# Sharing the first layer's weight conversion between ScalarE and VectorE in three ways

## The chip, the cores and the metric

One core of a Trainium2 chip. The metric is the device time of one execution in microseconds (us), the lower the better. TensorE multiplies matrices, ScalarE and VectorE work elementwise, GpSimd takes some elementwise work too, and SyncE's queue issues the DMA transfers.

## The reference, cut to what matters

```
attention (8 batches, 8 heads, 576 queries, 64 wide, 32 packed queries p):
    pp  = softmax(p k^T / 8) v            # 32 rows per head
    x   = softmax(q pp^T / 8) pp          # 4608 tokens x 512
layer 1:  h = x @ w_in;  g = h - tanh(h);  x = g @ w_out      # 512 -> 2048 -> 512
layer 2:  h = x @ w_in2; g = h * cos(h);   out = g @ w_out2   # float32
```

The weights arrive as 64-bit floats. The kernel has to make 32-bit floats of them on the chip, and splits each (as it does other operands) into a high part of type fp32r, which TensorE multiplies, and a low part, the rest, of the same type.

## The kernel before, in words

**Weights of layer 1.** `w_in` and `w_out` come as 16 tiles each, 32 in all, of 128 x 512 doubles (512 KB). `ORDER` (line 33) fixes their order; `i` is a tile of `w_in`, `o` one of `w_out`. The class `Conv` (line 105) takes a tile through stages. `prefetch` issues its load into the tile `st`, through SyncE's queue. `a` does ScalarE's part on the two 32-bit words of each double: line 140 scales the high word, read as a float, into the tile `w` (exponent and upper fraction bits, three places too low); line 142 makes the three lowest bits of the result from the low word; in one of two ways line 147 makes the sign. `b_ops` returns VectorE's part as a list of functions. `c` (only for `w_out`) splits into high part (ScalarE, line 185) and low part (GpSimd, line 186).

There were two ways. If `ACT_SIGN` has a 1 for the tile, line 142 writes the low bits into the lower 16-bit half of the low word and line 147 the sign, as a 16-bit float, into its upper half; VectorE then has one operation, `join` (line 164): shift `w` left by three and OR the word to it. If it has a 0, line 142 writes the whole 32-bit word, line 147 falls away, and VectorE puts in the sign (line 159) and then joins (line 164). The first 17 tiles and every second one after are of the first kind: 24 and 8. The weights of layer 2 take the second way, all of them, and much later.

**Steps.** Layer 1 runs in steps. A step is two of 16 groups of 128 hidden columns for one block of 288 tokens: `h1` (12 matmuls, line 459), `el1` (tanh and square on ScalarE, lines 474, 475), `el2` (VectorE, lines 486 to 493, with two ScalarE passes, 481 and 484), `el3` and `el4` (high part on ScalarE, line 501, and low part on VectorE, line 506), and two steps later `ymm1` (24 matmuls, line 521). VectorE's conversion functions go between those of `el2` (`fill`, line 997). `x @ w_in` is never made as such: `gmat` (line 413) multiplies the packed attention rows of a batch with `w_in` first, which needs four converted tiles of `w_in`, and `gsplit` (lines 435, 440) splits the product. The first 16 steps need the first half of both weights, the next ones the rest. The tables `PRE_A`, `PRE_B` and `STEP_A` say how many tiles are begun at each place of the program.

**Order.** The program first works on the attention of batch 0 with conversions between (`slot`), then runs the steps with the later batches' attention between them. Up to step 15 a scheduler orders each engine's queue when the program is built: by what is ready after its own durations, and by priority (the last part of batch 0's softmax has a higher one). From step 15 on each queue has the written order (`STEP_ORDERED`, line 42). Queues are served in order: an instruction that waits holds up all behind it on its engine. Scores, transposes, `gmat` and `h1` share two PSUM buffers (`psh`), and staged weights, converted weights and `gsplit`'s output share 32 buffers of the pool `wp`.

```
way "1":  ACT 140 high -> w     ACT 142 low bits -> 16-bit half   ACT 147 sign -> other half   DVE 164 join
way "0":  ACT 140 high -> w     ACT 142 low bits -> 32-bit word   DVE 159 sign                 DVE 164 join
```

Of the kernel before, what the change touches and what calls it, by code (L numbers as in the profile page):

```python
# [15 lines left out]
U32 = mybir.dt.uint32  # L16
F16 = mybir.dt.float16
BF16 = mybir.dt.bfloat16
AF = mybir.ActivationFunctionType
ALU = mybir.AluOpType  # L20
# [13 lines left out]
    "i2 i0 i3 i1 o1 o0 i4 i5 i6 i7 o3 o4 o2 o5 o7 i8 "  # L34
    "o6 i9 i10 i11 i14 o9 i12 i13 o8 i15 o11 o13 o12 o10 o15 o14"
).split()
ACT_SIGN = "11111111111111111010101010101010"
PRE_A = (0, 1, 1, 1, 1, 0, 1, 1, 1, 0, 1, 1, 0, 0, 0)
PRE_B = (1, 0, 1, 1, 2, 0, 2, 2, 0, 1, 2, 2, 0, 3, 0)
STEP_A = (1, 2, 2, 2, 1, 2, 1, 1, 1, 1, 0, 2, 1, 1, 1, 1, 1, 1, 0, 3, 1, 1)  # L40
# [12 lines left out]
SGN = -2147483648  # L53
LOW_BIAS = -0.5 + 2.0 ** -10
# [3 lines left out]
def fused_kernel(ctx, tc, qT, kT, v, pT, w1i, w1o, w2i, w2o, ident, out):  # L58
    nc = tc.nc
    B, _, _, _, HB = qT.shape  # L60
    S = 2 * HB
# [31 lines left out]
    def f32(ap):  # L93
        return ap.bitcast(F32)
# [10 lines left out]
    class Conv:  # L105
# [19 lines left out]
        def a(self):  # L125
            self.prefetch()
            if not self.ready:
                return
            kind, f, st = self.ready.pop(0)
            by_act = kind[1] == "1" and ACT_SIGN[self.na] == "1"  # L130
            self.na += 1
            if kind == "w1i":
                if f // 2 not in w1in:
                    w1in[f // 2] = wp.tile([128, 2, 512], F32, tag="w", name="w1i")
                w = w1in[f // 2][:, f % 2, :]
            else:
                w = self.alloc_tmp()
            sv = st.rearrange("p (n two) -> p n two", two=2)
            hi, x = sv[:, :, 1], sv[:, :, 0]
            nc.scalar.activation(out=w, in_=f32(hi), func=AF.Copy, scale=2.0 ** -112)  # L140
            halves = st.bitcast(U16).rearrange("p (n four) -> p n four", four=4)
            nc.scalar.activation(  # L142
                out=halves[:, :, 0] if by_act else x, in_=x.bitcast(U32), func=AF.Identity,
                scale=2.0 ** -29 * (1 - 2.0 ** -11), bias=LOW_BIAS,
            )
            if by_act:
                nc.scalar.activation(  # L147
                    out=halves[:, :, 1].bitcast(F16), in_=f32(hi), func=AF.Copy, scale=2.0 ** -60
                )
            self.done_a.append((kind, f, hi, w, x, by_act))  # L150

        def b_ops(self):
            if not self.done_a:
                return []
            kind, f, hi, w, x, by_act = self.done_a.pop(0)
            wi = w.bitcast(I32)

            def sign():
                nc.vector.scalar_tensor_tensor(
                    out=x, in0=hi, scalar=SGN, in1=x, op0=ALU.bitwise_and, op1=ALU.bitwise_or  # L160
                )

            def join():
                nc.vector.scalar_tensor_tensor(
                    out=wi, in0=wi, scalar=3, in1=x,
                    op0=ALU.logical_shift_left, op1=ALU.bitwise_or,
                )
                if kind == "w1i":
                    self.bdone.add(f)
                else:  # L170
                    self.done_b.append((kind, f, w))
                self.prefetch()

            return [join] if by_act else [sign, join]

        def b(self):
            for fn in self.b_ops():
# [563 lines left out]
    def bprep(t, bo):  # L741
# [16 lines left out]
        def sub(o, a, b):  # L758
            return lambda: nc.vector.tensor_tensor(out=o(), in0=a(), in1=b(), op=ALU.subtract)
# [273 lines left out]
    p3c, p3 = run_pool("p3")  # L1033
    pend, hist, bo, nyt, sums = [], [], {}, [], []
    seq = [(i, t, s, a, b) for i, (t, a, b) in enumerate(PARTS) for s in range(a, b)]
    nxt = [p[0] for p in PARTS[1:]]

# [200 lines left out]
```

## Time and profile before

| | |
|---|---|
| median of 3 runs | 1560.5 us (1559.47 to 1560.88) |
| profiled execution | 1559.06 us, its span 1557.2 us |
| TensorE busy | 1485.1 us (95%) |
| VectorE busy | 1115.0 us (72%) |
| ScalarE busy | 960.8 us (62%) |
| GpSimd busy | 184.4 us (12%) |

```profile
PE   3588999999999999999989999999999999999999
DVE  4598888787888878788965655567767577747661
```

The page cuts the span into 40 slices of 39 us and gives the busy share of each in tenths. TensorE is below 90% in the first four slices only. The conversion of layer 1 lies in the first five. PE is TensorE's matrix multiplication, PEld its weight load, DVE VectorE, ACT ScalarE, POOL GpSimd; PEclk is the granted clock of TensorE as a share of 2.4 GHz. Busy time counts each moment once, while the mean of a group counts an instruction's whole duration, and neighbours overlap by some 0.1 us.

### The profile page before, as it was taken

How to read it: one execution, taken by the hardware profiler on the slowest of the kernel's cores; microseconds unless marked ns; L12 is line 12 of the kernel's file. 1: busy time of each engine (PE TensorE's matmuls, PEld its weight loads, DVE VectorE, ACT ScalarE, POOL GpSimd, SP SyncE). 2: the span in 40 equal slices, each digit the busy share in tenths (PEclk: the TensorE clock that was granted, in tenths of full speed). 3: DMA queues.
4: the chain of work that ended last, by engine and by line, in shares of the span. 5: the costliest groups of instructions: out<-in, count | busy, mean ns of one | idle time of the engine just before them, and what ended most of it. 6: DMA issues, size and time to landing. Idle time of an engine off the chain costs nothing.

```text
span 1557.2 us, 25930 instructions
## 1 busy us (share of the span) xinstructions
PE 1485.1 (95%) x10192; PEld 1294.2 (83%) x10192; DVE 1115.0 (72%) x1547; ACT 960.8 (62%) x1450; POOL 184.4 (12%) x155
## 2 busy tenths in 40 slices
PE   3588999999999999999989999999999999999999
PEld 1477888999999999999978778888888888888887
DVE  4598888787888878788965655567767577747661
ACT  7998856565666757567877755555555355535541
POOL 0231101010100101011124435300000000000000
PEclk6699999999999999999999999999999999999999
DMA  9332223111212111103546742564666475647542
GB/s 342 134 130 84 92 67 106 35 62 62 66 62 64 43 37 50 62 32 113 170 144 228 239 167 95 198 233 167 236 226 259 140 257 188 260 151 280 177 172 110
DMA packets 88506, 223.54 MB, mean 144 GB/s; under 512 B 8960, under 2 KB 36608, under 8 KB 88384
## 3 DMA queue, kind: packets, MB, share of 16 engines
q1 hardware_dynamic: 88384, 221.88, 40.9%
q8 instruction: 81, 1.33, 0.4%
q14 instruction: 41, 0.34, 0.1%
HBM read 173.34 MB, written 48.50 MB: 142 GB/s over the span
## 4 chain that ended last, share of the span: by engine, by line
PE 84%; ACT 7%; DVE 4%; issue 3%; DMA 1%; POOL 1%; SPq 0%; DVEq 0%; POOLq 0%; ACTq 0%
PE y L642 24%; PE y L521 23%; PE p L791 15%; PE h L459 11%; PE h L585 7%; PE gp L421 2%; ACT st L142 2%; ACT st L147 1%; DVE y L489 1%; ACT wt L140 1%; PE pp L328 1%; DVE y L493 1%; ACT u L475 1%; DMA st<-w1i 1%; PE s L271 1%
## 5 line engine op out<-in xcount | busy, mean ns | idle before, releaser
L521 PE MATMUL y<-gh,w1o 128*128 128x288 f32 x2048 | 311.8, 304 | 11.3 <-ACT gh L501 6.3
L521 PEld LDWEIGHTS y<-gh,w1o 128*128 128x128 f32 x2048 | 285.2, 191 | 39.7 <-ACT t L474 14.5
L459 PE MATMUL h<-a,g 128*128 128x288 f32 x1536 | 229.3, 298 | 11.7 <-DVE g L440 6.3
L791 PE MATMUL p<-b,wa 128*128 128x512 f32 x1008 | 239.8, 389 | 0.0
L459 PEld LDWEIGHTS h<-a,g 128*128 128x128 f32 x1536 | 214.4, 191 | 14.4 <-ACT a L379 10.0
L791 PEld LDWEIGHTS p<-b,wa 128*128 128x128 f32 x1008 | 189.2, 188 | 39.2
L474 ACT ACTIVATE t<-h 128x576 f32<-128x576 f32 x128 | 83.6, 653 | 201.4 <-PE h L459 201.2
L642 PE MATMUL y<-wo,gh 128*128 128x512 f32 x768 | 188.1, 389 | 0.0
L642 PEld LDWEIGHTS y<-wo,gh 128*128 128x128 f32 x768 | 144.2, 188 | 29.9
L521 PE MATMUL y<-gl,w1o 128*128 128x288 f32 x1024 | 157.6, 296 | 0.5 <-DVE gl L506 0.5
L521 PEld LDWEIGHTS y<-gl,w1o 128*128 128x128 f32 x1024 | 143.2, 189 | 0.7 <-DVE gl L506 0.7
L486 DVE TENSOR_TENSOR t<-h,t 128x576 f32<-128x576 f32 x128 | 95.4, 745 | 59.7 <-ACT u L475 59.2
L585 PE MATMUL h<-yhl,w2i 128*128 128x512 f32 x576 | 134.3, 389 | 0.0
L585 PEld LDWEIGHTS h<-yhl,w2i 128*128 128x128 f32 x576 | 108.1, 188 | 22.4
L493 DVE COPY_PREDICATED y<-k,t 128x576 f32<-128x576 int16 x128 | 109.2, 854 | 12.5 <-DVE y L489 0.5
L802 ACT ACTIVATE a<-ha 128x1024 f32<-128x1024 f32 x24 | 25.5, 1062 | 140.3 <-DVE ha L799 140.3
L506 DVE TENSOR_TENSOR gl<-y,gh 128x576 fp32r<-128x576 f32 x128 | 102.0, 797 | 8.8 <-ACT gh L501 7.9
L642 PE MATMUL y<-w2o,gh 128*128 128x512 f32 x384 | 95.7, 395 | 3.9 <-DVE o L685 2.0
L489 DVE SCALAR_TENSOR_TENSOR y<-y,d 128x576 f32<-128x576 f32 x128 | 96.9, 757 | 2.3 <-ACT y L481 2.1
L642 PE MATMUL y<-wo,gl 128*128 128x512 f32 x384 | 97.8, 389 | 0.0
L487 DVE TENSOR_TENSOR d<-u,h 128x576 f32<-128x576 f32 x128 | 95.0, 742 | 0.0
L501 ACT ACTIVATE gh<-y 128x576 fp32r<-128x576 f32 x128 | 87.8, 686 | 9.1 <-DVE y L493 8.7
(116 smaller groups left out, 2118.3 us busy)
## 6 DMA issues: line engine op xcount, KB each, us to landing
wo<-wod SPq DMA_DIRECT2D x96, 512.0 KB, 6.2
wa<-wsd SPq DMA_DIRECT2D x48, 512.0 KB, 6.3
wa<-wid SPq DMA_DIRECT2D x24, 512.0 KB, 5.7
y<-ye SPq DMA_DIRECT2D x80, 144.0 KB, 1.9
out<-o SPq DMA_DIRECT2D x36, 256.0 KB, 2.2
st<-w1i SPq DMA_DIRECT2D x16, 512.0 KB, 8.0
v<-vv SPq DMA_DIRECT2D x16, 512.0 KB, 5.1
st<-w1o SPq DMA_DIRECT2D x16, 512.0 KB, 6.6
```

Of the source, the lines that this page charges most:

```text
L459: nc.tensor.matmul(out=h[:, x, 0:HB], lhsT=gw[b, f // 4, half][:, ga, c0:c0 + 128], rhs=a2[b, half][:, aa, HB * j:HB * j + HB], start=(n = ...
L474: nc.scalar.activation(out=st["t"], in_=h, func=AF.Tanh)
L486: lambda: nc.vector.tensor_tensor(out=t, in0=hs, in1=t, op=ALU.subtract),
L487: lambda: nc.vector.tensor_tensor(out=d, in0=u, in1=hs, op=ALU.mult),
L489: lambda: nc.vector.scalar_tensor_tensor(out=y, in0=y, scalar=PC0 - PC1 * PC1 / (4 * PC2), in1=d, op0=ALU.add, op1=ALU.mult,),
L493: lambda: nc.vector.copy_predicated(out=y, mask=k.bitcast(I16), data=t),
L501: nc.scalar.activation(out=st["gh"], in_=st["g"], func=AF.Copy)
L506: nc.vector.tensor_tensor(out=st["gl"], in0=st["g"], in1=f32(st["gh"]), op=ALU.subtract)
L521: nc.tensor.matmul(out=yps[blk][d][:, 0:HB], lhsT=w1out[f][:, wh, 128 * d:128 * d + 128], rhs=st[gg][:, x, :], start=(s in first and x == ...
L585: nc.tensor.matmul(out=h[:, x, :], lhsT=w2in[f][:, wa, 128 * k:128 * k + 128], rhs=yt[k][:, ya, :], start=(n == 0), stop=(n == 11),)
L642: nc.tensor.matmul(out=yps[t, lo_s][m], lhsT=st[gg][:, x, 128 * m:128 * m + 128], rhs=w[:, wh, :], start=(s == lo_s and x == 0 and not lo ...
L791: nc.tensor.matmul(out=dst, lhsT=wa[wi][:, 128 * j:128 * j + 128], rhs=b[j][:, bi, :], start=(n == 0), stop=(n == 5),)
```

## The change

A third way is added, and a string names the way of each tile: `S` is the old way 1, `L` the old way 0, and in `D` ScalarE only makes the high word; VectorE shifts it left by three in place (`shift`), puts in the sign (`put_sign`) and joins the top three bits of the untouched low word (`join`, its other branch). Of the 32 tiles 6 are S, 20 L and 6 D.

```diff
@@ -34,7 +34,7 @@
     "i2 i0 i3 i1 o1 o0 i4 i5 i6 i7 o3 o4 o2 o5 o7 i8 "
     "o6 i9 i10 i11 i14 o9 i12 i13 o8 i15 o11 o13 o12 o10 o15 o14"
 ).split()
-ACT_SIGN = "11111111111111111010101010101010"
+SPLIT = "LLSLLLSLLLSLLLSLDLSLDLDLSLDLDLDL"
 PRE_A = (0, 1, 1, 1, 1, 0, 1, 1, 1, 0, 1, 1, 0, 0, 0)
 PRE_B = (1, 0, 1, 1, 2, 0, 2, 2, 0, 1, 2, 2, 0, 3, 0)
 STEP_A = (1, 2, 2, 2, 1, 2, 1, 1, 1, 1, 0, 2, 1, 1, 1, 1, 1, 1, 0, 3, 1, 1)
@@ -127,7 +127,7 @@
             if not self.ready:
                 return
             kind, f, st = self.ready.pop(0)
-            by_act = kind[1] == "1" and ACT_SIGN[self.na] == "1"
+            way = SPLIT[self.na] if kind[1] == "1" else "L"
             self.na += 1
             if kind == "w1i":
                 if f // 2 not in w1in:
@@ -139,20 +139,21 @@
             hi, x = sv[:, :, 1], sv[:, :, 0]
             nc.scalar.activation(out=w, in_=f32(hi), func=AF.Copy, scale=2.0 ** -112)
             halves = st.bitcast(U16).rearrange("p (n four) -> p n four", four=4)
-            nc.scalar.activation(
-                out=halves[:, :, 0] if by_act else x, in_=x.bitcast(U32), func=AF.Identity,
-                scale=2.0 ** -29 * (1 - 2.0 ** -11), bias=LOW_BIAS,
-            )
-            if by_act:
+            if way != "D":
+                nc.scalar.activation(
+                    out=halves[:, :, 0] if way == "S" else x, in_=x.bitcast(U32),
+                    func=AF.Identity, scale=2.0 ** -29 * (1 - 2.0 ** -11), bias=LOW_BIAS,
+                )
+            if way == "S":
                 nc.scalar.activation(
                     out=halves[:, :, 1].bitcast(F16), in_=f32(hi), func=AF.Copy, scale=2.0 ** -60
                 )
-            self.done_a.append((kind, f, hi, w, x, by_act))
+            self.done_a.append((kind, f, hi, w, x, way))
 
         def b_ops(self):
             if not self.done_a:
                 return []
-            kind, f, hi, w, x, by_act = self.done_a.pop(0)
+            kind, f, hi, w, x, way = self.done_a.pop(0)
             wi = w.bitcast(I32)
 
             def sign():
@@ -160,18 +161,34 @@
                     out=x, in0=hi, scalar=SGN, in1=x, op0=ALU.bitwise_and, op1=ALU.bitwise_or
                 )
 
+            def shift():
+                nc.vector.tensor_scalar(
+                    out=wi, in0=wi, scalar1=3, scalar2=None, op0=ALU.logical_shift_left
+                )
+
+            def put_sign():
+                nc.vector.scalar_tensor_tensor(
+                    out=wi, in0=hi, scalar=SGN, in1=wi, op0=ALU.bitwise_and, op1=ALU.bitwise_or
+                )
+
             def join():
-                nc.vector.scalar_tensor_tensor(
-                    out=wi, in0=wi, scalar=3, in1=x,
-                    op0=ALU.logical_shift_left, op1=ALU.bitwise_or,
-                )
+                if way == "D":
+                    nc.vector.scalar_tensor_tensor(
+                        out=wi, in0=x, scalar=29, in1=wi,
+                        op0=ALU.logical_shift_right, op1=ALU.bitwise_or,
+                    )
+                else:
+                    nc.vector.scalar_tensor_tensor(
+                        out=wi, in0=wi, scalar=3, in1=x,
+                        op0=ALU.logical_shift_left, op1=ALU.bitwise_or,
+                    )
                 if kind == "w1i":
                     self.bdone.add(f)
                 else:
                     self.done_b.append((kind, f, w))
                 self.prefetch()
 
-            return [join] if by_act else [sign, join]
+            return {"S": [join], "L": [sign, join], "D": [shift, put_sign, join]}[way]
 
         def b(self):
             for fn in self.b_ops():
```

## Rows read from the trace of the kernel before

**Rows 1.** the stretches: busy us and instructions of each engine, PEclk, DMA share, GB/s

```profile
20.00:64.00 44.00, 14.76 (x131) 8.28 (x124) 26.74 (x47) 42.56 (x56) 7.29 (x5) 0.50 0.58 215
64.00:122.00 58.00, 45.47 (x422) 40.87 (x421) 49.67 (x73) 54.21 (x83) 16.32 (x11) 0.91 0.40 133
122.00:186.00 64.00, 59.68 (x492) 54.57 (x490) 55.62 (x79) 55.86 (x100) 9.59 (x7) 0.96 0.29 98
186.00:280.00 94.00, 89.82 (x912) 81.90 (x911) 80.53 (x136) 57.36 (x102) 8.80 (x7) 1.00 0.28 84
...
100.00:120.00 20.00, 15.57 (x137) 13.80 (x138) 19.27 (x31) 19.57 (x33) 6.80 (x5) 0.92 0.39 136
```

**Rows 2.** the chain of waits, 26 to 64 us: share by line

```profile
by line: ACT st L147 29.0%; ACT st L142 28.1%; PE y L521 6.7%; ACT wt L140 6.4%; ACT g L435 5.1%; ACT w1i L140 4.9%; ACT u L362 3.3%; ACT a L379 2.8%; ACT w1o L185 2.2%; ACT e L295 2.2%; DVE wt L164 1.8%; ACT gh L501 1.5%; ACT k L484 1.5%; 
```

**Rows 3.** TensorE's instructions in order: start, us, what, idle before and its releaser

```profile
40.88 3.22 PE L459 MATMUL h<-a,g 128*128 128x288 f32 x12 [6.33 <-DVE g L440]
54.39 1.96 PE L421 MATMUL gp<-w1i,pt 64*32 64x256 f32 x32 [10.29 <-ACT e L295]
...
63.86 2.66 PE L459 MATMUL h<-a,g 128*128 128x288 f32 x12
```

**Rows 4.** ScalarE's instructions in order

```profile
39.85 1.38 ACT L147 ACTIVATE st<-st 128x512 f16<-128x512 f32 x1
40.94 1.44 ACT L142 ACTIVATE st<-st 128x512 uint16<-128x512 uint32 x1
42.09 0.71 ACT L185 ACTIVATE w1o<-wt 128x512 fp32r<-128x512 f32 x1
...
54.24 0.64 ACT L474 ACTIVATE t<-h 128x576 f32<-128x576 f32 x1
...
88.27 0.69 ACT L140 ACTIVATE w1i<-st 128x512 f32<-128x512 f32 x1
88.84 0.68 ACT L142 ACTIVATE st<-st 128x512 int32<-128x512 uint32 x1
89.40 0.67 ACT L481 ACTIVATE y<-u 128x576 f32<-128x576 f32 x1
```

**Rows 5.** groups of 0 to 330 us by form: count, busy us, mean ns, idle before

```profile
L142 ACT ACTIVATE st<-st 128x512 uint16<-128x512 uint32 x24 | 32.8, 1380 | 0.0
...
L147 ACT ACTIVATE st<-st 128x512 f16<-128x512 f32 x24 | 32.6, 1369 | 0.2
...
L164 DVE SCALAR_TENSOR_TENSOR wt<-wt,st 128x512 int32<-128x512 int32 x16 | 14.0, 879 | 6.9 <-ACT st L147 3.3 <-ACT wt L140 2.7 <-DMA st<-w1o 0.8
L164 DVE SCALAR_TENSOR_TENSOR w1i<-w1i,st 128x512 int32<-128x512 int32 x16 | 11.8, 747 | 13.4 <-ACT st L147 9.4 <-ACT w1i L140 4.0
...
L159 DVE SCALAR_TENSOR_TENSOR st<-st 128x512 int32<-128x512 int32 x8 | 8.7, 1085 | 0.9 <-ACT st L142 0.9
...
L142 ACT ACTIVATE st<-st 128x512 int32<-128x512 uint32 x8 | 5.6, 705 | 0.0
```

**Rows 6.** all engines in order, 119.3 to 120.1 us

```profile
119.37 0.68 DVE L164 SCALAR_TENSOR_TENSOR w1i<-w1i,st 128x512 int32<-128x512 int32 x1
...
119.84 1.50 POOL L380 TENSOR_TENSOR a<-ut,a 128x576 fp32r<-128x576 f32 x1 [6.00 <-ACT a L379]
119.97 1.93 DVE L159 SCALAR_TENSOR_TENSOR st<-st 128x512 int32<-128x512 int32 x1
```

**Rows 7.** VectorE's one-input operations of the whole span

```profile
L685 DVE TENSOR_SCALAR o<-y 128x512 f32<-128x512 f32 x18 | 12.3, 687 | 19.9 <-PE y L642 9.6 <-POOL w2o L186 8.3 <-DMA out<-o 2.0
...
L338 DVE TENSOR_SCALAR px<-pp,sm 128x128 f32<-128x128 f32 x16 | 5.5, 341 | 4.5 <-PE pp L328 4.5
```

**Rows 8.** the sign passes (line 147) by stretch: busy us and count

```profile
0.00:54.20 54.20, 16.06 (x12) 0.64 0.81 292
...
64.00:122.00 58.00, 10.90 (x8) 0.91 0.40 133
122.00:186.00 64.00, 4.22 (x3) 0.96 0.29 98
```

## The prediction, made before the result was known

> **What bounds the kernel now.** I read the busy time by stretch first [rows 1]. From 186 us on TensorE is busy 89.8 of 94 us; nothing in this change happens there, so what counts is how much earlier or later the steps reach that stretch. Before it, in 20 to 186 us, the fullest engine is ScalarE: 42.56 of 44 us (97%), 54.21 of 58 (93%) and 55.86 of 64 (87%). VectorE has 26.74 (61%), 49.67 (86%) and 55.62 (87%). TensorE does little up to 64 us, and at a granted clock of 0.50, its 1.2 GHz level; from 64 to 122 us it is idle for 12.5 us.
>
> Then the chain of waits of 26 to 64 us [rows 2]: lines 147 and 142, ScalarE's sign and low-bits passes of the conversion, are 57% of it. TensorE's rows show what that does [rows 3]: the first h product runs at 40.88, and then TensorE waits 10.29 us for ScalarE's exp of batch 1 (which frees a PSUM buffer); the first tanh starts only at 54.24 [rows 4], though its product is done at 44.1. The second h product starts at 63.86.
>
> **What a tile costs on each engine.** By form [rows 5] the low-bits pass takes 1380 ns into the 16-bit half and 705 ns into the 32-bit word; the sign pass, 16-bit too, 1369 ns. Neighbours overlap, so I take start to start [rows 4]: sign 40.94-39.85 = 1.09, 16-bit low bits 42.09-40.94 = 1.15, high bits 88.84-88.27 = 0.57, 32-bit low bits 89.40-88.84 = 0.56. So a tile holds ScalarE for 0.57+1.15+1.09 = 2.81 us by way S, 1.13 by L, 0.57 by D.
>
> On VectorE S has one op (join), L two, D three. The two ops that exist take 680 ns undisturbed, 0.60 start to start (119.37 to 119.97) [rows 6]. But over all 40 of them the mean is (16x879 + 16x747 + 8x1085)/40 = 867 ns [rows 5], since some are stretched; less the 0.08 of overlap, 0.79 each. The sign op at 119.97 shows the stretch: 1.93 us while GpSimd's L380 runs (119.84 for 1.50) [rows 6]. The Trainium skill, "SBUF — State Buffer", section "SBUF: two separate sides", says that a VectorE op with two SBUF inputs and a GpSimd op exclude each other for a whole instruction. Rows 6 agree, and it speaks against the change: 18 of the added ops have two SBUF inputs.
>
> The shift of way D has no row: a one-input op of 512 elements, SBUF to SBUF. The nearest row is the 512-element scalar op out of PSUM, 687 ns [rows 7]; below it lies nothing but the op's fixed part, for which the 128x128 row (341 ns) is an upper bound. I take the same 0.79 as for the others; with 0.34 six shifts would save 2.7 us of VectorE, and that end I keep for the range. The Trainium skill, "VectorE: DVE Perf Modes", section "The perf-mode tier table", gives such an fp32 op two elements a cycle; by it the sum would be about 2 us lower (an estimate), and no row here shows that.
>
> **The change, stretch by stretch.** Sign passes: 24 in all [rows 5], 8 and 3 of them in the second and third stretch [rows 8], so 13 in the first; since before every tile up to number 16 and the even ones after are S, these are tiles 0-12, 13-25 and 26-31.
> - Up to 64 us: tiles 0,1,3,4,5,7,8,9,11,12 go S to L. ScalarE 10 x 1.68 = -16.8; VectorE +10 ops = +7.9.
> - 64 to 122: tiles 13, 15 to L, 16, 20, 22 to D. ScalarE 2x1.68 + 3x2.24 = -10.1; VectorE 2+6 = 8 ops, +6.3.
> - 122 to 186: tiles 26, 28, 30 to D. ScalarE -6.7; VectorE 6 ops, +4.7.
>
> Sum: ScalarE -33.6, VectorE +18.9 us. Loads, their queue, the high/low split (lines 185, 186) and TensorE's work stay as they are.
>
> Start. Twelve sign passes lie ahead of the first tanh at 54.24 [rows 8], nine of them on tiles that become L: ScalarE would be free for it 9x1.68 = 15.1 us earlier, at 39.1. The product it reads then ends last (44.1; it waits for VectorE's g and ScalarE's a, which I put 3 us earlier, so 41). So ScalarE's side would give 13 us. VectorE's side gives less: 26.74+7.9, less some 1.6 us (signs of tiles 0 and 1, whose low bits are made before 20 us) = 33.0 us of work. Filled as ScalarE was here, 97%, that takes 34.0 instead of 44 us: **-10.0**. The smaller gain counts.
>
> After it VectorE is the fullest engine. 64 to 122: 49.67+6.3 = 56.0; filled as ScalarE now is, 93%, it takes 60.2: **+2.2**. 122 to 186: 55.62+4.7 = 60.4, at the same 93% 64.9: **+0.9**. There is a row for such filling: 19.27 of 20 us (96%) in 100 to 120. TensorE needs less than that in the second stretch (45.47 busy), and about the same in the third (59.68).
>
> Sum -6.9 on the profiled execution's 1559.06 (span 1557.2 and 1.9 around it): 1552.2. The median of the runs is 1.4 above the profiled one, so 1553.5.
>
> What hides what: the added VectorE ops cost nothing only where VectorE waits for ScalarE (17 us idle in 20 to 64). If the static order sets them ahead of batch 0's softmax or of the maximum of batch 1, that cover is gone and each costs its 0.8. From step 15 the order is the written one: a D tile puts three ops between the chain's ops of a step instead of one, so the masked copy that ends it (and with it gh, y's operand) comes up to 1.6 us later; with 93% filling that is counted.
>
> **Rivals.**
> 1. *The order closes up* (22%). The passes that go were what the start waited for, and with ScalarE 20% emptier VectorE no longer waits for it: the start gives the 13 us of ScalarE's side, and the 116.4 us of VectorE work in 64 to 186 fit at 98%, 118.8 against 122. -16: 1544.5. For it: a queue as full as ScalarE's, 93 to 97%, is what each release had to pass through. Against it: 98% stands in no row.
> 2. *VectorE too full, slower* (20%). VectorE in 64 to 186 fills only as in 186 to 280, where nothing else is full: 80.53 of 94, 86%; TensorE is 4% idle there already. And the added ops meet GpSimd as the eight old sign ops did (1085 ns, 1.0 each), for GpSimd is busy 28% of 64 to 122. Then 105.3+14.0 = 119.3 at 88% is 135.6, +13.6, while the start gives 26.74+10-2 = 34.7 at 93%, 37.3, -6.7. +7: 1567; with 90% +4, 1564. It decides from below 90% filling on. For it: both engines were nearly even here and the load only changes place.
> 3. *The start is held elsewhere* (13%). Between the first tanh and the second h product 9.6 us pass through two PSUM buffers (gp of rows 3, then a transpose and scores of batch 1); if the order puts the freed time of ScalarE to later tiles instead, the start gives the 3 us of the first product only, and VectorE takes them back: within 0.2%, 1557.4 to 1563.6, which is about what a measurement can tell from no change. DMA is no such holder: busy 0.58 of 20 to 64 [rows 1].
>
> That the passes don't get shorter is excluded: 1380 against 705 ns in one line and one kernel.
>
> **How the numbers follow.** My forecast has 45%, 1553.5, its own range 1548 to 1557 (95% and 91% filling, with the shift's two ends). The rivals have 22, 20 and 13%. Faster 67%, same 13%, slower 20%. The range goes from 1542 (rival 1 with the cheap shift) to 1565 (most of rival 2).
>
> **What would show it.** In the profile after: sign passes 24 to 6, 16-bit low bits 24 to 6, 32-bit low bits 8 to 20; ScalarE some 40 us less busy, VectorE 15 to 19 more; first tanh near 42 and second h product near 54; in 64 to 175 VectorE over 92% and ScalarE under 80%. Wrong if the second h product stays near 64 (rival 3), if VectorE stays under 90% while TensorE's idle time grows after it (rival 2), or if the second stretch shortens too (rival 1). From 186 us on (by the new clock 7 earlier) everything should be as before.

## The result, and the profile after

The median is 1543.86 us (5 runs) against 1559.97 us: ratio 0.9898, 95% interval 0.9883 to 0.9912, 16 us less. Forecast were 7 us less (1553.5); the direction and the start came as forecast, the size of what follows the start did not, and the time is that of rival 1. The profiled execution took 1545.49 us, its span is 1543.6, so the traces show 13.6 of the 16 us.

In the new listing the conversion's ScalarE passes are lines 140 (high), 143 (low bits) and 148 (sign), VectorE's operations 160 (sign), 181 (join), and 165, 170, 176 (way D); all behind stands 17 lines lower. Of the page after: part 1, and two rows of part 2 (slices of 38.6 us).

```profile
PE 1486.3 (96%) x10192; PEld 1293.5 (84%) x10192; DVE 1124.2 (73%) x1571; ACT 927.1 (60%) x1426; POOL 185.2 (12%) x155
...
PE   4889999999999999999989999999999999999999
...
DVE  5899888787878878788956655567767577747661
```

VectorE's busy time over the whole run rose by 9.2 us (1115.0 to 1124.2); forecast were 15 to 19. ScalarE's fell by 33.7, which is the sum's 33.6 and not the "some 40" of its last paragraph. In 64 to 175 us VectorE is 94% busy and ScalarE 79%, as that paragraph had it.

The stretches are best cut where the same step starts: at the second h product (steps are counted from 0, so this is step 1), at that of step 9 and that of step 17. Columns as in [rows 1]: PE, PEld, VectorE, ScalarE, GpSimd, then granted clock, DMA share, GB/s. The kernel before:

```profile
20.00:63.90 43.90, 14.66 (x131) 8.18 (x124) 26.64 (x47) 42.46 (x56) 7.29 (x5) 0.50 0.58 215
63.90:128.70 64.80, 52.27 (x461) 46.58 (x461) 55.05 (x81) 58.50 (x92) 17.61 (x12) 0.88 0.36 119
128.70:171.90 43.20, 40.10 (x349) 37.02 (x347) 37.49 (x52) 39.14 (x68) 5.70 (x4) 1.00 0.33 113
```

The changed one:

```profile
20.00:55.00 35.00, 15.46 (x124) 8.69 (x125) 31.63 (x55) 27.72 (x48) 7.15 (x5) 0.50 0.71 264
55.00:114.70 59.70, 50.81 (x458) 44.92 (x458) 55.15 (x87) 48.01 (x82) 17.22 (x12) 0.88 0.37 130
114.70:157.50 42.80, 40.02 (x350) 37.09 (x348) 40.52 (x58) 35.11 (x65) 6.49 (x5) 1.00 0.36 117
```

So the three stretches shrank by 8.9, 5.1 and 0.4 us; forecast were -10.0, +2.2 and +0.9. (The forecast cut at 122 and 186 us, not at steps 9 and 17; with the nearest marks, the last matmuls of step 8's h and step 19, the second shrank by 5.0 and the third by 0.6.) VectorE's work in them (the third busy column) is 26.64, 55.05, 37.49 before and 31.63, 55.15, 40.52 after: +5.0, +0.1, +3.0, where I had +6.3, +6.3 and +4.7. Its filling is 90, 92 and 95%, where I had 97, 93 and 93%. From step 17 on 0.8 us are lost again.

The groups of 0 to 330 us by form, against [rows 5]:

```profile
L160 DVE SCALAR_TENSOR_TENSOR st<-st 128x512 int32<-128x512 int32 x20 | 15.7, 795 | 0.2 <-ACT st L143 0.2
L143 ACT ACTIVATE st<-st 128x512 int32<-128x512 uint32 x20 | 13.7, 683 | 0.1
...
L181 DVE SCALAR_TENSOR_TENSOR w1i<-w1i,st 128x512 int32<-128x512 int32 x14 | 10.6, 771 | 3.4 <-ACT w1i L140 3.4
...
L181 DVE SCALAR_TENSOR_TENSOR wt<-wt,st 128x512 int32<-128x512 int32 x12 | 9.3, 779 | 0.0
...
L143 ACT ACTIVATE st<-st 128x512 uint16<-128x512 uint32 x6 | 8.2, 1364 | 0.0
L148 ACT ACTIVATE st<-st 128x512 f16<-128x512 f32 x6 | 8.2, 1360 | 0.1
...
L165 DVE TENSOR_SCALAR wt<-wt 128x512 int32<-128x512 int32 x4 | 2.9, 736 | 0.0
...
L170 DVE SCALAR_TENSOR_TENSOR wt<-st,wt 128x512 int32<-128x512 int32 x4 | 2.7, 678 | 0.0
L176 DVE SCALAR_TENSOR_TENSOR wt<-st,wt 128x512 int32<-128x512 int32 x4 | 2.7, 677 | 0.0
...
L170 DVE SCALAR_TENSOR_TENSOR w1i<-st,w1i 128x512 int32<-128x512 int32 x2 | 1.8, 908 | 0.0
...
L176 DVE SCALAR_TENSOR_TENSOR w1i<-st,w1i 128x512 int32<-128x512 int32 x2 | 1.4, 681 | 0.0
...
L165 DVE TENSOR_SCALAR w1i<-w1i 128x512 int32<-128x512 int32 x2 | 0.8, 410 | 0.0
```

The sign pass fell from 24 to 6, the low bits in 16-bit form from 24 to 6, as read off the diff. The shift that no row showed takes 410 ns where nothing disturbs it.

### The profile page after: what moved, and what is told of

Read it like the earlier page. It is cut to its first block, busy times and chain, and to the rows that moved or that the text cites. A ratio compares the mean times of both kernels' runs of the same rounds, so it can differ in the third digit from the quotient of the medians.

```text
span 1543.6 us, 25927 instructions
## 1 busy us (share of the span) xinstructions
PE 1486.3 (96%) x10192; PEld 1293.5 (84%) x10192; DVE 1124.2 (73%) x1571; ACT 927.1 (60%) x1426; POOL 185.2 (12%) x155
## 4 chain that ended last, share of the span: by engine, by line
PE 86%; DVE 6%; ACT 4%; issue 3%; DMA 1%; POOL 1%; SPq 0%; DVEq 0%; ACTq 0%; POOLq 0%
PE y L659 24%; PE y L538 24%; PE p L808 15%; PE h L476 11%; PE h L602 7%; PE gp L438 2%; DMA v<-vv 1%; DVE y L510 1%; PE pp L345 1%; DVE st L160 1%; DVE y L506 1%; ACT st L143 1%; DVE t L503 1%; PE s L288 1%; PE sc L288 1%
## 5 line engine op out<-in xcount | busy, mean ns | idle before, releaser
L503 DVE TENSOR_TENSOR t<-h,t 128x576 f32<-128x576 f32 x128 | 95.4, 745 | 59.7 <-ACT u L492 59.0
```

Of the source, the lines that this page charges most:

```text
L503: lambda: nc.vector.tensor_tensor(out=t, in0=hs, in1=t, op=ALU.subtract),
```

## The experiments

Each kernel is the changed one unless another is named, its median set against runs of the kernel before on the same chip.

**Tiles 0 to 12 alone, and tiles 13 to 31 alone.**

```diff
-SPLIT = "LLSLLLSLLLSLLLSLDLSLDLDLSLDLDLDL"
+SPLIT = "LLSLLLSLLLSLLSSSSLSLSLSLSLSLSLSL"   # e1: 13 to 31 as before
+SPLIT = "SSSSSSSSSSSSSLSLDLSLDLDLSLDLDLDL"   # e2: 0 to 12 as before
```

> Only tiles 0 to 12 take their new way; tiles 13 to 31 keep the old one. Theory V (VectorE is the bound after the start, at about 93% filling, and an added VectorE operation costs 0.6 us, because the stretch by GpSimd belongs to GpSimd's operations and not to VectorE's): the second h product comes near 55 and all of it stays, 9 to 10 us under the kernel before, 1550 to 1551. Theory S (ScalarE's passes were on the path everywhere, VectorE has room): the start alone gives its share, 9, and ScalarE still holds the second stretch: also 1551. By the forecast's prices: 1550. Below 1547 all three are wrong and the order matters.

> Only tiles 13 to 31 take their new way (ScalarE 17 us less, VectorE 14 operations more); the start is that of the kernel before, second h product near 64. Forecast's prices (0.79 an operation): 3 us slower than before, 1563. Theory V (0.6 an operation): VectorE gets 7 us more work in a stretch where it and ScalarE were nearly even: 0 to 3 us faster, 1557 to 1560. Theory S: 5 to 8 us faster, 1552 to 1555.

Measured: e1 1551.33 us, 0.9947 (0.9932 to 0.9962), 8.3 us less; e2 1557.77, 0.9988 (0.9979 to 0.9998), 1.9 us less. e1 parts no theory (it lies 0.3 us above all of them), e2 lies in V's span. Together they give 10, and the whole change gives 16: the second part is worth 2 us on the old start and 7.5 on the new one. No theory had said that; it showed that the sum of stretches, each with its own bound, leaves something out.

**VectorE's sign twice; ScalarE's sign pass kept.** Both repeat what is there, the result of the OR is the same.

```diff
-            return {"S": [join], "L": [sign, join], ...
+            return {"S": [join], "L": [sign, sign, join], ...        # e3, layer 1 only
...
-            if way == "S":
+            if way == "S" or (way == "L" and kind[1] == "1"):        # e4
                 nc.scalar.activation(out=halves[:, :, 1].bitcast(F16), ...
```

> The changed kernel, with VectorE's sign operation done twice in the 20 L tiles (the second OR changes nothing): 20 VectorE operations more, at 0.6 us 12 us of work, ScalarE as it was. Theory V: 8 to 12 us slower than the changed kernel, 1552 to 1556, and GpSimd's stretch of VectorE's operations in total stays near 6.5 us. Theory S: 0 to 4 us slower, 1544 to 1548.

> The changed kernel, with ScalarE's sign pass done as well in the 20 L tiles (VectorE ORs the same sign again): 20 passes of 1.09 us more on ScalarE, 22 us, VectorE as it was. Theory V: the start loses 6 to 9 us, the rest next to nothing: 1550 to 1553. Theory S: all of the gain goes, 1558 to 1562.

Measured: e3 1552.85 us, 0.9954 (0.9937 to 0.9971), 9.0 above the changed kernel, as theory V had it. e4 1556.85, 0.9973 (0.9964 to 0.9982), 13.0 above it: more than V allowed, less than S. e4's ten runs lie in two groups, four at 1553.2 to 1554.4 and six at 1556.8 to 1557.2; the lower one is at the edge of V's span. (These are medians from different chips. By the ratios to the kernel before, e3 is 8.7 and e4 11.7 us above the changed kernel.) Twelve us more on VectorE cost 9, 22 us more on ScalarE 12 to 13. So neither engine is the bound by itself. e4 is not a test of ScalarE alone: its ScalarE is 23.1 us busier than in the changed kernel, and its VectorE, without an operation more, 6.7. Theory Q was formed here: until about step 5 the queues of both lie on the path, because each serves in order and each chain of a step changes between them several times; later the conversion costs little.

The group of VectorE's signs in e3:

```profile
L160 DVE SCALAR_TENSOR_TENSOR st<-st 128x512 int32<-128x512 int32 x40 | 32.4, 819 | 0.3 <-ACT st L143 0.2
```

**Tiles 0 to 16, 17 to 31 as before; no D; VectorE's added work left out; VectorE's added work alone.**

```diff
+SPLIT = "LLSLLLSLLLSLLLSLDLSLSLSLSLSLSLSL"                           # e5
+SPLIT = "LLSLLLSLLLSLLLSLLLSLLLLLSLLLLLLL"                           # e6
...
+            return {"S": [join], "L": [join], "D": [join]}[way]      # e7, layer 1 only
...
+SPLIT = "AASAAASAAASAAASABLSLBLBLSLBLBLBL"                           # e8: A, B with all of S's passes
+            ... "A": [sign, join], "B": [sign, sign, join]}[way]
```

> Tiles 0 to 16 take their new way, tiles 17 to 31 the old one. The two halves of the change alone gave 8.3 and 1.9 us, 10 together, the whole 16; the missing 6 lie in steps 1 to 5 (20 us in the changed kernel, 27 with only tiles 0 to 12), where tiles 13 to 16 are converted. Theory Q (until about step 5 the queues of both engines are on the path, whatever their filling; later the conversion costs little): nearly all of the gain, 1544 to 1547. Theory V (VectorE's work over a filling of 93%): the VectorE operations of tiles 17 to 31 that go save some 6 us, 1537 to 1541. Theory S (ScalarE's passes everywhere on the path): 1549 to 1552.

> The changed kernel with way L in place of D in its six tiles: ScalarE six passes of 0.56 us more, VectorE a shift of 0.33 to 0.6 us less in each. All theories: within 2 us of the changed kernel, 1542 to 1546; 1547 or more would say that even ScalarE's short passes late in the conversion are on the path.

> The changed kernel without VectorE's sign operations: L tiles only join, D tiles only join too (shift and sign left out, so the signs and low bits of those weights are missing); 20 + 12 VectorE operations less, 17 us of work, ScalarE as it was. Theory Q: the ten signs ahead of step 1 and the few up to step 5 come off the path at some 0.5 us each, 1536 to 1540. Theory V: 17 us over 0.93, 1526 to 1530. Theory S: 1541 to 1544.

> The kernel before, ScalarE's work untouched, with the 24 VectorE operations that the change adds (the sign ORed in once more in 12 tiles, twice in 6): 14 us of VectorE work. Theory Q: in the start VectorE waits for ScalarE and hides its ten, up to step 5 a few count, 1561 to 1564. Theory V: VectorE becomes as full as ScalarE, 1564 to 1570. Theory S: no change, 1559 to 1561.

Measured: e5 1546.51 us, 0.9922 (0.9905 to 0.9938); e7 1537.54, 0.9859 (0.9844 to 0.9874), 6.3 below the changed kernel (6.1 by the ratios); e8 1563.28, 1.0028 (1.0017 to 1.0040), 3.1 above the kernel before (4.4 by the ratio). The medians of all three lie where theory Q put them, though three of e8's eight runs (up to 1567.88) lie in V's span; V is refuted by each of e5 and e7, S by e5, e7 and e8. e6, 1540.84 (0.9885, 0.9871 to 0.9900), came 1 us under what any theory had.

The three stretches of e8 (step 1 at 65.2, step 9 at 130.3, step 17 at 175.9):

```profile
20.00:65.20 45.20, 16.67 (x155) 8.66 (x140) 33.42 (x54) 43.73 (x57) 7.71 (x5) 1.00 0.55 209
65.20:130.30 65.10, 52.92 (x458) 46.23 (x458) 55.35 (x85) 58.26 (x90) 14.91 (x12) 0.87 0.36 119
130.30:175.90 45.60, 40.66 (x351) 37.49 (x351) 42.99 (x61) 39.80 (x69) 8.13 (x5) 1.00 0.33 111
```

ScalarE is as full as before, 97% in the first and 89% in the second, VectorE 74 and 85%. VectorE has 6.8 us more work in it than before and the stretch is 1.3 us longer: what ScalarE makes it wait for hides the rest. e8 has VectorE's added operations and not ScalarE's saving; the step from it to the changed kernel is ScalarE's 33.6 us, beside D's six shifts in place of six ORs (VectorE is 6.0 us less busy over the whole run), and is worth 19.4.

Where tiles 13 to 16 matter, 55 to 75 us, first with them as before (e1), then by their new ways (e5):

```profile
55.00:75.00 20.00, 16.50 (x172) 15.63 (x171) 15.64 (x24) 17.14 (x26) 3.09 (x2) 0.91 0.43 142
```

```profile
55.00:75.00 20.00, 19.23 (x217) 17.51 (x216) 18.91 (x31) 18.80 (x33) 6.61 (x4) 1.00 0.59 206
```

TensorE is busy for 16.50 of the 20 us with the sign passes, 19.23 without, and VectorE, which has more to do in e5, does more too: 18.91 against 15.64. Of the 4.4 us that VectorE stands idle in e1, it waits 2.8 for ScalarE and 1.3 for TensorE.

One wait can be followed, before the third h product. In e1:

```profile
63.02 0.69 DVE L181 SCALAR_TENSOR_TENSOR wt<-wt,st 128x512 int32<-128x512 int32 x1 [1.15 <-ACT st L148]
63.49 3.09 POOL L203 TENSOR_TENSOR w1o<-wt,w1o 128x512 fp32r<-128x512 f32 x2 [8.68 <-ACT w1o L202]
63.63 1.83 DVE L506 SCALAR_TENSOR_TENSOR y<-y,d 128x576 f32<-128x576 f32 x1
65.49 1.74 DVE L510 COPY_PREDICATED y<-k,t 128x576 f32<-128x576 int16 x1
67.52 3.25 PE L476 MATMUL h<-a,g 128*128 128x288 f32 x12 [3.50 <-DVE px L355]
```

In e5, and the same product in e2:

```profile
61.75 0.68 DVE L181 SCALAR_TENSOR_TENSOR wt<-wt,st 128x512 int32<-128x512 int32 x1
62.36 0.82 DVE L510 COPY_PREDICATED y<-k,t 128x576 f32<-128x576 int16 x1
64.02 1.85 PE L476 MATMUL h<-a,g 128*128 128x288 f32 x12 [0.48 <-DVE px L355]
```

```profile
77.81 3.25 PE L476 MATMUL h<-a,g 128*128 128x288 f32 x12 [3.85 <-DVE px L355]
```

In e1 a join waits for a sign pass, and the step's own operations stand behind it in VectorE's queue. Two of them then run beside GpSimd's operations and take 1.83 and 1.74 us; `px` (line 355), which frees the PSUM buffer, comes last. TensorE waits 3.50 us for it, and then the 12 matmuls take 3.25 us at a granted clock of 0.50 (67.5 to 70.8 us), its 1.2 GHz level; in e5 it waits 0.48 us, and they take 1.85 at 1.00. e2, on the old start, still has the wait (3.85 us), though its tile 13 takes the new way. From step 1 to step 5 e1 needs 27.0 us and e5 19.6; this wait and the slow matmuls behind it are some 4 of the 7.4.

All that the second stretch gains lies there: from step 1 to step 5 the kernel before needs 26.6 us and the changed one 20.1, from step 5 to step 9 they need 38.2 and 39.6.

**Once more, on one chip: the changed kernel, the one without D, all tiles by L, and tiles 7 and 8 by S.**

```diff
+SPLIT = "LLSLLLSLLLSLLLSLLLSLLLLLSLLLLLLL"   # e10
+SPLIT = "LLLLLLLLLLLLLLLLLLLLLLLLLLLLLLLL"   # e11
+SPLIT = "LLSLLLSSSLSLLLSLLLSLLLLLSLLLLLLL"   # e12
```

> The changed kernel once more, on one chip with the three that follow: 0.9898 of the kernel before, 1543 to 1545. All theories agree.

> Way L in place of D once more, beside the changed kernel on one chip. If the 3 us of the first time are real: 1540 to 1542, and VectorE's third operation late in the conversion has a price; if not, 1543 to 1545.

> All 32 tiles by way L: against the one with L for D, ScalarE six times 1.68 us less, VectorE six signs more, three of each up to step 1. Theory Q (both queues on the path up to step 5): the two nearly cancel, 1539 to 1543. Theory V: 3 to 4 us slower than with six S, 1544 to 1546. Theory S: 5 to 9 us faster, 1532 to 1536.

> L for D, and tiles 7 and 8 by way S: two VectorE signs fewer ahead of batch 1's maximum, which is late on VectorE while ScalarE waits 3.9 us for it, and 3.4 us more on ScalarE ahead of it. Theory Q: within 2 us of the one with L for D, 1539 to 1543. Theory V: 1 to 2 us faster, 1538.5 to 1540. Theory S: 2 to 4 us slower, 1543 to 1545.

Measured: e9 1544.64 us (1543.27 to 1546.03), 0.9902 (0.9888 to 0.9917); e10 1540.46 (1540.23 to 1541.30), 0.9876 (0.9862 to 0.9891); e11 1540.41, 0.9878 (0.9863 to 0.9892); e12 1542.14, 0.9886 (0.9869 to 0.9902). The runs of e9 and e10 don't overlap (their ratios' intervals do, by 0.0003), and e6's highest (1543.40) lies above the lowest of the changed kernel's first runs (1542.88) and below their median: the kernel without D is 3 to 4 us faster than the changed one, by two repeats that agree. With all tiles by L the time is the same and the code simpler; these two are the best versions found. S in six tiles or in none makes no difference, which V and S both excluded; e12 lies in Q's span, though its runs (1540.63 to 1543.01) reach the edge of S's.

Where D loses: TensorE in the changed kernel, and in e10, about step 17.

```profile
153.62 1.23 PE L538 MATMUL y<-gl,w1o 128*128 128x288 f32 x8
157.53 2.83 PE L476 MATMUL h<-a,g 128*128 128x288 f32 x12 [2.69 <-DVE d L504]
```

```profile
152.75 1.23 PE L538 MATMUL y<-gl,w1o 128*128 128x288 f32 x8
155.20 1.82 PE L476 MATMUL h<-a,g 128*128 128x288 f32 x12 [1.23 <-DVE d L504]
```

In both the h product waits for VectorE's `d` (line 504), which is what frees its PSUM buffer; with two D tiles in the steps ahead it waits 2.69 us, with L 1.23, and after the longer wait the 12 matmuls take 2.83 us instead of 1.82: the granted clock is 0.62 in 157 to 161 us of the changed kernel, so part of it is at the 1.2 GHz level, and 1.00 in 155 to 157 of e10. From step 15 to step 18 the changed kernel needs 20.5 us, e10 18.2, which is 2.3 of the 4 us.

## Why the prediction was right in part

1. **What bounds the kernel, right.** Rows 2 gave ScalarE's passes 57% of the chain ahead of 64 us. In the changed kernel the chain of 20 to 55 us, by line, is

```profile
by line: DVE w1i L181 11.3%; issue 10.6%; PE y L538 8.6%; ACT st L143 8.4%; DVE st L160 8.3%; ACT w1i L140 4.6%; ACT st L148 3.8%; PE tp L326 3.8%; ACT u L379 3.6%; DVE u L367 3.4%; ACT wt L140 3.2%; ACT g L452 2.8%; ACT e L312 2.4%; DVE ut
```

   and lines 143 and 148 have 12% of it. TensorE after, against [rows 3]:

```profile
36.51 0.58 PE L476 MATMUL h<-a,g 128*128 128x288 f32 x1 [2.70 <-DVE g L457]
39.39 1.33 PE L476 MATMUL h<-a,g 128*128 128x288 f32 x4 [2.30 <-ACT a L396]
41.24 2.05 PE L476 MATMUL h<-a,g 128*128 128x288 f32 x7 [0.52 <-POOL a L397]
45.87 1.96 PE L438 MATMUL gp<-w1i,pt 64*32 64x256 f32 x32 [2.58 <-ACT e L312]
...
55.01 2.00 PE L476 MATMUL h<-a,g 128*128 128x288 f32 x12
```

   The wait of 10.29 us for the exp of batch 1 is 2.58.

2. **The start, right with the smaller of two numbers.** Forecast 10.0 us, VectorE's side; measured 8.9 (63.86 to 55.01). That VectorE would hold it can be seen in its rows and in ScalarE's:

```profile
36.97 2.32 DVE L160 SCALAR_TENSOR_TENSOR st<-st 128x512 int32<-128x512 int32 x2
39.22 2.52 DVE L181 SCALAR_TENSOR_TENSOR w1i<-w1i,st 128x512 int32<-128x512 int32 x2
41.66 1.28 DVE L160 SCALAR_TENSOR_TENSOR st<-st 128x512 int32<-128x512 int32 x2
42.86 0.68 DVE L181 SCALAR_TENSOR_TENSOR w1i<-w1i,st 128x512 int32<-128x512 int32 x1
43.47 0.74 DVE L304 TENSOR_REDUCE nm<-sc 128x1 f32<-128x576 f32 x1
```

```profile
40.34 0.70 ACT L140 ACTIVATE wt<-st 128x512 f32<-128x512 f32 x1
44.99 0.74 ACT L312 ACTIVATE e<-sc,nm 128x576 f32<-128x576 f32 x1 [3.95 <-DVE nm L305]
...
45.72 0.64 ACT L491 ACTIVATE t<-h 128x576 f32<-128x576 f32 x1
```

   Seven conversion operations stand ahead of batch 1's maximum (line 304), some stretched; ScalarE waits 3.95 us for it and the first tanh starts at 45.72, not at 42. The 97% filling that I took for VectorE was too full, 90% came; the work was smaller too (31.63, not 33.0). These two errors partly cancel (31.63 at 97% would be 32.6 us, 33.0 at 90% 36.7; measured 35.0), so that the size came within 1.1 us is in part luck.

3. **The second stretch, the step that failed.** The term was "64 to 122: 49.67+6.3 = 56.0; filled as ScalarE now is, 93%, it takes 60.2: +2.2". The filling came as taken, 92%. The added work was mis-sized: VectorE has 0.1 us more by steps, not 6.3. So the step that failed is that each operation given to VectorE makes the full VectorE longer by its 0.79 us. With 55.15 us at 93% the term is 59.3 of 64.8, -5.5; measured -5.1. That is 7.3 us apart, where the sum is 6.7 apart (-6.9 against -13.6 in the traces); the other terms nearly cancel. Three things were in the 6.3:
   - I charged every added operation with the stretch that the old ones showed, 0.19 us. It does not go with their number. By the groups' means over 680 ns (410 for the shift), the conversion's operations were stretched by 7.5 us in 40 operations before and by 6.5 in 64 after; from all of their groups, by 9.1 in 84 in e3 (theory V had 6.5), 9.3 in 64 in e8, 6.6 in 32 in e7 and 11.7 in 64 in e4. GpSimd's work is the same in all of them (184 to 185 us), and e4 has the very operations of the changed kernel: how often they meet GpSimd's is a matter of order and timing. The rule of the Trainium skill that I weighed ("SBUF — State Buffer", section "SBUF: two separate sides"), by which the one that starts first runs through and the other waits, was seen at work: in e1 GpSimd's operation starts at 63.49 and VectorE's at 63.63 takes 1.83 us. It says who waits, not how often.
   - The shift takes 0.41, not 0.79 (three of them in this stretch).
   - The conversion's own 25 operations in that stretch took 18.5 us, the 19 before 15.7, so six more (not eight) and +2.7; VectorE's other work there fell by as much. The largest part is the masked copy: before, three of its eight ran beside an operation of GpSimd (1.86, 1.76 and 1.46 us, the others 0.81 to 0.83), after it one (1.47). Before and after:

```profile
L493 DVE COPY_PREDICATED y<-k,t 128x576 f32<-128x576 int16 x8 | 9.2, 1149 | 0.3 <-ACT k L484 0.3
L510 DVE COPY_PREDICATED y<-k,t 128x576 f32<-128x576 int16 x8 | 7.1, 892 | 0.0
```

   The low part `gl` took 0.6 us more; the rest I can't name.

4. **The model under it, wrong as well.** I let the fullest engine's work over a filling set each stretch. By e4 and e8 ScalarE's time is worth 0.5 to 0.6 us a us (11.7 to 13.0 for 22; 19.4 for 33.6), while VectorE's is worth 0.2 to 0.3 when ScalarE is full (e8: 3.1 to 4.4 for 14), 0.7 when it is not (e3: 9.0 for 12), and 0.4 when it is taken away (e7: 6.3 for 17, of which only 11.2 show in VectorE's busy time). These are rough prices, since in each of these kernels the stretches and the order moved as well. Two engines that pass work to and fro through queues in order both set the pace here; freeing one shortens a stretch although the other has as much to do as ever. That is what the second stretch shows: VectorE's work 55.05 and 55.15 us, 64.8 and 59.7 long.

5. **The third stretch, right within 1.3 us** (+0.9, measured -0.4), **and D.** The text said that a D tile would bring the masked copy up to 1.6 us later and counted that in the filling. It costs more: e10 gains 4 us without it, 2.3 of them where it waits for `d`, as shown above.

6. **Rival 1** has the right time (1544.5), and the sign that was named for it, that the second stretch shortens too, is what came. Not quite its reasons: the start gave 8.9, not 13, and VectorE filled to 92%, not 98%; its work in the second stretch did not grow, which rival 1 had not said either. That its time fits so closely is luck in part. Rival 2's filling of 86 to 90% did not come with an emptier ScalarE; rival 3's start is excluded.

What stays open: how all of the 5.6 us that the two halves give only together divide among waits. From e1 to e5 tiles 13 to 16 bring 4.8 us (3.9 by the ratios), and the one wait followed above, with the slow matmuls behind it, is most of that; the rest is told by theory Q and not shown. A rival to Q was not parted from it: up to step 15 the scheduler makes a new order for every kernel, for the steps' own operations too. Of ScalarE's some 125 instructions ahead of step 15 that are not conversion, and VectorE's some 140, the traces show 19 and 12 in another order in e5 than in e1 (for one step e1 has `gh` ahead of line 498, e5 behind it), 15 and 9 in the changed kernel than in the one before, 12 and 4 in e3 than in the changed kernel, and none in e9. No run held the order and changed the work alone, or the other way round. A queue order that sets batch 1's maximum ahead of the seven operations was not run.

## What to carry to other kernels

Where two engines stretch each other's operations, don't carry the mean stretch of the old operations over to added ones: here the total was 6.5 to 11.7 us for the same 64 operations and 6.6 for 32: it went with order and timing, not with the number. Where two engines in series are both nearly full, price work moved between them by doing it twice (the idempotent operation repeated, the old pass kept) on each side, since neither busy share says what a us of it is worth; and look in the profile after whether the other engine's work stayed as it was. And several small operations between a step's own ones can cost more than the pass that they save, as D did: it spared ScalarE, 82% busy in the third stretch, and loaded VectorE, 95% busy.

## What the runs showed of the hardware

A ScalarE pass of 128x512 that writes 16-bit elements 8 bytes apart takes 1360 to 1380 ns, with 32-bit elements at the same distance 683 to 705 ns. And the granted clock of a stretch is to be read beside what the matmuls took in it. In 20 to 55 us the profile gives 0.50 (1.2 GHz) for the changed kernel and 1.00 (2.4 GHz) for the same kernel in e9, but the same seven matmuls of h take 2.05 us in both, here in e9:

```profile
42.23 2.05 PE L476 MATMUL h<-a,g 128*128 128x288 f32 x7 [0.48 <-POOL a L397]
```

Later, at 1.00, twelve take 1.74 (0.15 us each, against 0.29). So the 1.00 that some profiles give for the start (e8's above too) is not the speed that its matmuls show. Step 1 starts at 55.01 in the one trace of this kernel and at 55.96 in the other: differences of 1 us in the start between single traces say nothing.
